# One level of Strassen's scheme for the last two token chunks of a fused attention and gated feed-forward kernel

## The chip, the cores and the metric

The kernel runs on one core of a Trainium2 chip. The metric is the device time of one execution in microseconds (us). Three timed runs of the kernel before took 415.01, 415.22 and 415.52 us; their median is 415.22 us. Engines are named as in the profile: PE (TensorE matmuls), PEld (its weight loads), DVE (VectorE), ACT (ScalarE), POOL (GpSimd), SP (SyncE, here a DMA queue).

## The reference, cut to what matters

```python
# q, k, v: (8 batches, 8 heads, 1152, 64) float32
q_pool = q.reshape(B, H, S // 2, 2, D).mean(axis=3)           # 576 queries per head
attn   = softmax(q_pool @ k.T / sqrt(D))
x      = (attn @ v).transpose(0, 2, 1, 3).reshape(B * S // 2, 512)   # 4608 tokens
# w1, w2: (512, 1024); w3: (1024, 1024); w_out: (1024, 512)
out    = ((x @ w1) * (x @ w2)) @ w3 @ w_out                     # float32, (4608, 512)
```

## The kernel before, in words

**Attention.** Heads are worked in 32 pairs. Scores (`scores`, L422 to L436) go to PSUM, ACT takes their exponential into a ring buffer in SBUF (L436), and `av_mm` (L449 to L464) multiplies the ring by `v`. DVE normalises (`av_norm`, L479 to L499). For later pairs a DMA transpose on the SP queue writes the result into `xT` (L473), the transposed attention output with 512 features on 4 x 128 partitions and tokens along the columns; the 64 tokens that are left of each batch are turned on PE and copied by DVE (L517).

**Feed-forward.** The product T = w3 @ w_out is formed early in the kernel (`t_groups`, L527; matmuls of 256 columns at L544) and is kept in fp16 as `T16`. Tokens are worked in 9 chunks of 512 (`moe_groups`, L582 to L639). For each of 8 feature tiles `ft`, `proj` (L563 to L567) makes 4 matmuls of 512 columns with `w1`, then 4 with `w2`. The first product is copied out of PSUM (`asb`: L593 on ACT once attention is over, L595 on DVE before that), and DVE multiplies the second one with it into `gT` in fp16 (L599). Then each of the 4 tiles of 128 tokens takes 8 matmuls of 512 columns against `T16` (L610), is scaled out of PSUM half by DVE (L616) and half by ACT (L617), and is stored. The last tile is cut into 384 and 128 columns (L623 to L634).

**Order.** A planner (`_Plan`, `_visits`) searches, before the program is emitted, in what order scores, AV units and feed-forward steps go on PE while attention runs. A chunk is put into the queue when its tokens exist (`release`, L754). The chunks are numbered from 0. Chunk 6 is worked beside the last attention units; chunks 7 and 8 come after all of them, in the stretch where attention is over (`tail`, L806 on).

**Queues.** POOL makes the casts and pair sums of the inputs (L343, L347, L349, L356) and issues the stores of chunks that are worked during attention; SP issues loads, the transposes of `xT`, and the stores of the tail; ACT issues the last two. Each engine takes its instructions in program order. PSUM has 8 banks of 512 fp32 columns: three tiles `psc` of two banks, one `mo`, and one `avb`.

**Checks.** The softmax sums are checked on DVE (L816 to L822), one small matmul adds the result up (L827), and a register is loaded from it (`values_load`, L833) ahead of a general path that isn't taken here.

Of the kernel before, what the change touches and what calls it, by code (L numbers as in the profile page):

```python
# [8 lines left out]
FP32 = mybir.dt.float32  # L9
FP16 = mybir.dt.float16  # L10
AF = mybir.ActivationFunctionType
ALU = mybir.AluOpType
# [109 lines left out]
class _Plan:  # L122
# [62 lines left out]
    def copy(self):  # L185
        p = _Plan.__new__(_Plan)
        p.__dict__.update(self.__dict__)
        return p
# [63 lines left out]
REACH = 1.5  # L252


@with_exitstack
def kernel(
    ctx: ExitStack,
# [10 lines left out]
    nc = tc.nc  # L268
# [14 lines left out]
    QM = 4  # L283
# [29 lines left out]
    wosb = msb.tile([128, NF, dm], FP16)  # L313
# [108 lines left out]
    def scores(s):  # L422
        psc = ps.tile([128, 2, 512], FP32, tag="psc", bufs=3, name="psc")
        f = s * G
        while f < s * G + G:
            p, r = f // FLAT, f % FLAT
            jt, i0 = r // Sq, r % Sq
            ln = min(Sq - i0, s * G + G - f)
            kT2, qpT = pairs[p][:2]
            for u in range(2):  # L430
                nc.tensor.matmul(psc[:, u, f - s * G:f - s * G + ln],  # L431
                                 kT2[u * 64:u * 64 + 64, jt, :], qpT[u * 64:u * 64 + 64, i0:i0 + ln],
                                 start=True, stop=True)
            f += ln
        r0 = (s * G) % RING
        nc.scalar.activation(out=ring[:, :, r0:r0 + G], in_=psc, func=AF.Exp, bias=0.0, scale=SCALE)  # L436
# [129 lines left out]
                nc.tensor.matmul(pw[:, d0:d0 + n], wt[:, mc, ft * 128:ft * 128 + 128], xT[:, mc, a:a + n],  # L566
                                 start=(mc == 0 and d0 == 0), stop=(mc == NC - 1), skip_group_check=True)  # L567

    def store(eng, pos, osb):
        b, r = pos // (2 * Sq) * 2, pos % (2 * Sq)  # L570
        if r == QM * 128:
            for u in range(2):
                r0 = (b + u) * Sq + QM * 128
                eng.dma_start(out=out[r0:r0 + QT, :], in_=osb[u * QT:u * QT + QT, :])
            return
        if r > QM * 128:
            b, r = b + 1, r - QM * 128 - 2 * QT
        eng.dma_start(out=out[b * Sq:b * Sq + QM * 128, :].rearrange("(p c) n -> p c n", c=QM)[:, r // 128, :], in_=osb)  # L578

    final, near = [], [False]  # L580

    def moe_groups(c):  # L582
        t = {}

        def first(pa, ft):
            if ft == 0:
                t["g"] = msb.tile([128, NF, CH], FP16, tag="g8", bufs=2, name="gT")
            proj(pa, w1sb, ft, c)

        def keep(pa):  # L590
            t["a"] = msb.tile([128, CH], FP32, tag="asb", bufs=2, name="asb")
            if tail[0]:
                nc.scalar.copy(out=t["a"], in_=pa)  # L593
            else:
                nc.vector.tensor_copy(out=t["a"], in_=pa)  # L595

        for ft in range(NF):
            def gate(pb, ft=ft):
                nc.vector.tensor_tensor(out=t["g"][:, ft, :], in0=pb, in1=t["a"], op=ALU.mult)  # L599
# [3 lines left out]
        tts = list(range(0, CH, 128))  # L603
        if c in final:
            tts.sort(key=lambda tt: (c * CH + tt) % (2 * Sq) != QM * 128)
        for n, tt in enumerate(tts):
            def go(po, tt=tt, n=n):
                near[0] = c in final and n >= len(tts) - 3
                for ft in range(NF):
                    nc.tensor.matmul(po, t["g"][:, ft, tt:tt + 128], T16[:, ft, :],  # L610
                                     start=(ft == 0), stop=(ft == NF - 1))

            def put(po, tt=tt):
                osb = msb.tile([128, dm], FP32, tag="osb", bufs=3)
                if tail[0]:
                    nc.vector.tensor_scalar_mul(out=osb[:, 0:256], in0=po[:, 0:256], scalar1=1.0 / (SCL * SCL))  # L616
                    nc.scalar.mul(out=osb[:, 256:512], in_=po[:, 256:512], mul=1.0 / (SCL * SCL))  # L617
                    store(nc.scalar if c in final and tt == tts[-2] else nc.sync, c * CH + tt, osb)
                else:
                    nc.vector.tensor_scalar_mul(out=osb, in0=po, scalar1=1.0 / (SCL * SCL))  # L620
                    store(nc.gpsimd, c * CH + tt, osb)

            def go_last(po, tt=tt):  # L623
                osb = msb.tile([128, dm], FP32, tag="osb", bufs=3)
                for hs in (slice(0, 384), slice(384, dm)):
                    ph = ps.tile([128, 2, 512], FP32, tag="psc", bufs=3, name="mol")[:, 0, 0:hs.stop - hs.start]
                    for ft in range(NF):
                        nc.tensor.matmul(ph, t["g"][:, ft, tt:tt + 128], T16[:, ft, hs],
                                         start=(ft == 0), stop=(ft == NF - 1))
                    if hs.start:  # L630
                        nc.scalar.mul(out=osb[:, hs], in_=ph, mul=1.0 / (SCL * SCL))
                    else:
                        nc.vector.tensor_scalar_mul(out=osb[:, hs], in0=ph, scalar1=1.0 / (SCL * SCL))
                store(nc.scalar, c * CH + tt, osb)  # L634

            if c in final and n == len(tts) - 1:
                yield 2, go_last, None, 0.0
            else:
                yield 2, go, put, 0.0  # L639

    queue, ahead = [], []

# [89 lines left out]
    final.extend(loose[max(loose)])  # L732
    units = []
    for i, (p, t) in enumerate(UNITS):
        old = p - 1 if t == QM else p
# [18 lines left out]
    def release():  # L754
        for c in loose.get(avn[0], []):
            queue.append(moe_groups(c))
# [70 lines left out]
    nc.tensor.matmul(avb[0:1, 0:1], okh, ones, start=True, stop=True)  # L827
# [3 lines left out]
    while not near[0]:  # L831
        fill()
    bad = nc.values_load(badi[0:1, 0:1], min_val=0, max_val=128 * NQ)  # L833
    while fill():
        pass
    fast.close()
    with tc.If(bad > 0):
        _general(tc, q, k, v, out, w1sb, w2sb, T16)
# [30 lines left out]
```

## Time and profile before

| what | value |
|---|---|
| median of the timed runs | 415.22 us (415.01 to 415.52) |
| span of the profiled execution, first to last instruction | 414.1 us |
| what lies around the span, median less span (the profiled execution has no other time on record) | 1.1 us |
| PE busy over the span | 399.9 us (97%) |
| ACT, DVE, POOL busy over the span | 78%, 50%, 40% |
| matmuls of chunks 7 and 8 in the chain that ended last | 367.68 to 409.36 us of the span |
| last instruction that the trace lists | a store issued at 409.69 us, 0.42 us long |

Read the page from its part 4, the chain that ended last: it names the engine on which time can be won or lost. Busy times of the other engines show what they could still take. A matmul's listed duration holds the time until its end is modelled, so neighbours overlap; the distance from one start to the next is what it costs PE. In the groups, "128x512 f16" after the names is the operand on each partition, and "128*128" marks the full array.

### The profile page before, as it was taken

What the parts mean: (1) busy time and instruction counts of PE and PEld (TensorE: products, weight loads), DVE (VectorE), ACT (ScalarE), POOL (GpSimd) and SP (SyncE); (2) the same over time, 40 slices, a digit from 0 to 9 for tenths busy, and PEclk for the clock granted to TensorE, in tenths of its full rate; (3) what the DMA queues carried; (4) which work ended last, traced back from release to release, by engine and by line L of the source; (5) the groups of instructions that cost most, each with busy time, mean ns of one, the idle gap of its engine ahead of it and who ended that gap; (6) DMA issues with size and microseconds to landing.
All of it is one profiled execution on the core that took longest, in us unless ns stands there. A gap on an engine that the chain in (4) does not pass through costs nothing.

```text
span 414.1 us, 12744 instructions
## 1 busy us (share of the span) xinstructions
PE 399.9 (97%) x5337; PEld 246.9 (60%) x5337; DVE 205.5 (50%) x573; ACT 323.4 (78%) x353; POOL 167.6 (40%) x212
## 2 busy tenths in 40 slices
PE   3899999999999999999999999999999999999995
PEld 1477787565556655566556556655777655644442
DVE  1256665665356535554455436553556346744241
ACT  4878979898989998899999999999899986022321
POOL 4979976470655316504535155505532210010000
PEclk9999999999999999999999999999999999999999
DMA  8999999999799898959999999998975440030302
GB/s 263 210 320 289 269 286 312 348 247 265 185 238 252 221 286 278 242 70 278 273 264 280 264 252 270 292 260 163 303 207 121 85 90 15 16 114 2 101 0 108
DMA packets 90832, 86.34 MB, mean 209 GB/s; under 512 B 59664, under 2 KB 64272, under 8 KB 90768
## 3 DMA queue, kind: packets, MB, share of 16 engines
q1 hardware_dynamic: 81312, 58.80, 59.1%
q0 software_dynamic: 8880, 25.63, 21.6%
q10 hardware_dynamic: 576, 1.05, 0.8%
q8 instruction: 42, 0.69, 0.7%
q14 instruction: 22, 0.18, 0.1%
HBM read 67.11 MB, written 9.44 MB: 185 GB/s over the span
## 4 chain that ended last, share of the span: by engine, by line
PE 93%; ACT 2%; DMA 2%; DVE 1%; issue 1%; SPq 0%; POOL 0%; ACTq 0%
PE psc L431 20%; PE avb L462 17%; PE mot L566 16%; PE mo L566 15%; PE mo L610 11%; PE mot L610 5%; PE mo L544 3%; PE avb L459 3%; ACT ring L436 2%; PE ptk L371 2%; DMA kst<-in_k_dram 2%; DVE kqT L373 1%; PE mot L544 1%; PE mo L535 1%; PE mot L535 1%
## 5 line engine op out<-in xcount | busy, mean ns | idle before, releaser
L436 ACT ACTIVATE ring<-psc 128x1024 f16<-128x1024 f32 x324 | 308.3, 1025 | 33.8 <-PE psc L431 32.0
L462 PEld LDWEIGHTS <-ring 128*128 128x128 f16 x2304 | 84.4, 98 | 26.3 <-issue 7.1
L431 PE MATMUL psc<-kqT 64*128 64x512 f16 (+7 forms) x1152 | 96.2, 291 | 3.4 <-ACT ring L436 0.9
L462 PE MATMUL avb<-vaug,ring 128*128 128x65 f16 x2304 | 91.4, 193 | 0.0
L343 POOL CAST kq<-kst 128x1152 f16<-128x1152 f32 x31 | 35.7, 1150 | 74.3 <-DMA kqT<-kq 52.3
L431 PEld LDWEIGHTS <-kqT 64*128 64x128 f16 x1152 | 46.0, 95 | 31.0 <-issue 8.4
L578 POOL DMA_DIRECT2D out_dram<-osb x23 | 12.7, 551 | 101.6 <-DVE rzall L483 99.9
L610 PE MATMUL mo<-T,gT 128*128 128x512 f16 x192 | 45.6, 380 | 0.0
L566 PEld LDWEIGHTS <-w2sb 128*128 128x128 f16 x320 | 28.2, 98 | 28.3 <-issue 4.2
L566 PEld LDWEIGHTS <-w1sb 128*128 128x128 f16 x320 | 28.2, 98 | 27.7 <-issue 3.9
L610 PEld LDWEIGHTS <-gT 128*128 128x128 f16 x280 | 25.3, 98 | 32.2 <-issue 5.2
L483 DVE RECIPROCAL rzall<-avb 128x2 f32<-128x2 f32 x144 | 23.8, 165 | 37.0 <-PE avb L462 20.2
L566 PE MATMUL mot<-xT,w1sb 128*128 128x512 f16 (+2 forms) x172 | 41.1, 364 | 0.1
L620 DVE TENSOR_SCALAR osb<-mo 128x512 f32<-128x512 f32 x24 | 16.6, 692 | 48.5 <-PE mo L610 48.5
L347 POOL TENSOR_TENSOR kq<-qst 128x512 f16<-128x512 f32 x31 | 39.4, 1272 | 1.2 <-DMA qst<-in_q_dram 1.2
L566 PE MATMUL mot<-xT,w2sb 128*128 128x512 f16 (+2 forms) x156 | 38.0, 368 | 0.0
L356 POOL CAST vaug<-vst 128x1152 f16<-128x1152 f32 x32 | 36.6, 1143 | 2.6 <-DMA vst<-in_v_dram 2.5
L599 DVE TENSOR_TENSOR gT<-mot,asb 128x512 f16<-128x512 f32 x37 | 25.6, 692 | 22.0 <-PE mot L566 20.8
L599 DVE TENSOR_TENSOR gT<-mo,asb 128x512 f16<-128x512 f32 x35 | 24.2, 692 | 24.6 <-PE mo L566 24.4
L566 PE MATMUL mo<-xT,w2sb 128*128 128x512 f16 (+2 forms) x164 | 36.2, 349 | 0.0
L595 DVE COPY asb<-mo 128x512 f32<-128x512 f32 x32 | 22.1, 691 | 24.0 <-PE mo L566 23.7
L566 PE MATMUL mo<-xT,w1sb 128*128 128x512 f16 (+2 forms) x148 | 33.1, 351 | 0.0
(76 smaller groups left out, 287.4 us busy)
## 6 DMA issues: line engine op xcount, KB each, us to landing
vst<-in_v_dram SPq DMA_DIRECT2D x25, 576.0 KB, 4.9
kst<-in_k_dram SPq DMA_DIRECT2D x23, 576.0 KB, 5.9
qst<-in_q_dram SPq DMA_DIRECT2D x23, 512.0 KB, 7.2
out_dram<-osb POOLq DMA_DIRECT2D x23, 256.0 KB, 5.2
kst<-in_k_dram POOLq DMA_DIRECT2D x8, 576.0 KB, 9.8
qst<-in_q_dram POOLq DMA_DIRECT2D x8, 512.0 KB, 10.4
vst<-in_v_dram POOLq DMA_DIRECT2D x7, 576.0 KB, 7.2
w3c<-in_moe_w_dram POOLq DMA_DIRECT2D x4, 512.0 KB, 8.1
```

Source lines behind the costliest of these rows:

```text
L343: nc.gpsimd.tensor_copy(out=kq16[:, 0:NJ].rearrange("p c u d -> p u c d"), in_=kst.rearrange("p u (c d) -> p u c d", d=D))
L347: eng.tensor_tensor(out=kq16[:, NJ:NJ + QM].rearrange("p c u d -> p u c d"), in0=qv[:, :, :, 0], in1=qv[:, :, :, 1], op=ALU.add)
L356: nc.gpsimd.tensor_copy(out=va[:, :, :, 0:D], in_=vs.pop(p).rearrange("p u (c d) -> p u c d", d=D))
L431: nc.tensor.matmul(psc[:, u, f - s * G:f - s * G + ln], kT2[u * 64:u * 64 + 64, jt, :], qpT[u * 64:u * 64 + 64, i0:i0 + ln], start=True, s ...
L436: nc.scalar.activation(out=ring[:, :, r0:r0 + G], in_=psc, func=AF.Exp, bias=0.0, scale=SCALE)
L462: nc.tensor.matmul(avb[:, o + u * E1:o + u * E1 + E1], ring[:, u, c0:c0 + 128], va[:, u, jt, :], start=(jt == 0 and u == 0), stop=(jt == N ...
L483: nc.vector.reciprocal(out=rzall[:, i, :], in_=av[:, :, D:E1].rearrange("p u o -> p (u o)"))
L566: nc.tensor.matmul(pw[:, d0:d0 + n], wt[:, mc, ft * 128:ft * 128 + 128], xT[:, mc, a:a + n], start=(mc == 0 and d0 == 0), stop=(mc == NC - ...
L595: nc.vector.tensor_copy(out=t["a"], in_=pa)
L599: nc.vector.tensor_tensor(out=t["g"][:, ft, :], in0=pb, in1=t["a"], op=ALU.mult)
L610: nc.tensor.matmul(po, t["g"][:, ft, tt:tt + 128], T16[:, ft, :], start=(ft == 0), stop=(ft == NF - 1))
L620: nc.vector.tensor_scalar_mul(out=osb, in0=po, scalar1=1.0 / (SCL * SCL))
```

## The change

For chunks 7 and 8 alone, each of the three products (x with w1, x with w2, the gated result with T) is cut into 2 x 2 blocks and formed from 7 block products instead of 8 (Winograd's form of Strassen's scheme). With A the stationary side and B the moving side:

- sums of blocks: S1 = A21 + A22, S2 = S1 - A11, S3 = A11 - A21, S4 = A12 - S2; T1 = B12 - B11, T2 = B22 - T1, T3 = B22 - B12, T4 = B21 - T2
- products: P1 = A11 B11, P2 = A12 B21, P3 = S4 B22, P4 = A22 T4, P5 = S1 T1, P6 = S2 T2, P7 = S3 T3
- results: C11 = P1 + P2; u2 = P1 + P6; u3 = u2 + P7; C21 = u3 + P4; C22 = u3 + P5; C12 = u2 + P5 + P3

The sums of products are held in PSUM as far as they go: bank x of a set collects P1, P6, P7, P4; bank y gets a copy of P1 made by ACT, to which P2 is added; bank z collects P5 and P3. ACT copies u2 and u3 out to SBUF on the way, and DVE adds them to z for C12 and C22.

A **unit** is one block product of a set: 4 matmuls of 256 columns. There are 8 sets for the projections ("g", two chunks x two groups j of feature tiles x two weights w) and 4 for the product with T ("o", two chunks x two groups u of tokens), of 7 units each: 84 units. Sets with w = 0 leave fp32 results in SBUF; sets with w = 1 multiply theirs into `gT`, and then form the four sums of `gT` that the product with T needs. These multiplications out of SBUF and sums go to POOL where j is even, to DVE where j is odd (`side`).

Sums of the weights and of T (12 instructions of 1024 fp16 elements a partition, `weight_sums`) go to POOL after its last cast; sums of x (8 of 512 elements, `x_sums`) go to POOL after the last attention unit. The stores of chunks 5 and 6 go from the POOL queue to SP. The last chunk's first 256 tokens are stored in two column halves, one of them on the ACT queue for one tile. A new search (`_Late.order`) gives the order of the 84 units on PE and their banks. The small matmul of the check comes ahead of the 84 units, and its register is loaded 6 units before their end. The old last-tile split is gone.

```diff
+class _Late:
+    UNIT = 0.436
+    SEEN = {"act": 0.2, "dve": 0.2, "pool": 0.25}
+    AFTER = {1: (), 5: (), 6: (1,), 2: (1,), 7: (6,), 4: (7,), 3: (7, 5)}
...
+    def order(sets, full, width=60, look=3):
...
+                    cost = n.pe - n.work + 0.1 * max(0, n.eng["dve"] - n.pe - 0.5) + 0.05 * max(0, n.eng["act"] - n.pe - 0.5)
...
+                store(nc.sync if c >= LATE - 2 else nc.gpsimd, c * CH + tt, osb)
...
+    def weight_sums():
+        for w, tag in ((w1sb, "kst"), (w2sb, "vst")):
...
+            nc.gpsimd.tensor_tensor(out=s1, in0=a21, in1=a22, op=ALU.add)
+            minus(s2, s1, a11)
+            minus(s3, a11, a21)
+            minus(s4, a12, s2)
...
+    def late_chunks(before_end):
...
+        sets = [("g", j, w) for j in range(4) for w in range(2)] + [("o", c, u) for c in range(2) for u in range(2)]
+        order, bank = _Late.order(sets, (0, 2, 4))
...
+            pt = banks[bank[k, {1: "x", 6: "x", 7: "x", 4: "x", 2: "y", 5: "z", 3: "z"}[p]]]
+            for f, l in enumerate(left):
+                for i in range(kc):
+                    nc.tensor.matmul(pt[:, n * f:n * f + n], l[:, i, :], b[:, i, :],
+                                     start=(p in (1, 5) and f == 0 and i == 0), stop=(i == kc - 1), skip_group_check=True)
...
+            def plus(c, pz, u):
...
+                nc.vector.tensor_tensor(out=slot((k, c)), in0=pz, in1=at[k, u], op=ALU.add)
+                if gated:
+                    side.tensor_tensor(out=part(k[1] // 2, last, i, n), in0=flat(at[k, c]), in1=flat(at[a, c]), op=ALU.mult)
...
+            if p == 1:
+                nc.scalar.copy(out=banks[bank[k, "y"]][:, 0:w], in_=pt[:, 0:w])
...
+                for o, x, y, op in ((s1, g12, g22, ALU.add), (s3, g11, g12, ALU.subtract),
+                                    (s2, s1, g11, ALU.subtract), (s4, g21, s2, ALU.subtract)):
+                    side.tensor_tensor(out=o, in0=x, in1=y, op=op)
...
-        loose.setdefault(min(n, NU + 1), []).append(c)
+        if c < LATE:
+            loose.setdefault(min(n, NU + 1), []).append(c)
...
+                    weight_sums()
...
+    x_sums()
...
-    for _ in range(12):
-        fill()
+    while fill():
+        pass
     nc.tensor.matmul(avb[0:1, 0:1], okh, ones, start=True, stop=True)
...
+    late_chunks(lambda: bads.append(nc.values_load(badi[0:1, 0:1], min_val=0, max_val=128 * NQ)))
```

More of the change, by code (lines that the diff above doesn't have):

```diff
@@ L252, with __init__, copy, op @@
 REACH = 1.5
+class _Late:
+    UNIT = 0.436
+    SEEN = {"act": 0.2, "dve": 0.2, "pool": 0.25}
+    AFTER = {1: (), 5: (), 6: (1,), 2: (1,), 7: (6,), 4: (7,), 3: (7, 5)}
+    def __init__(self, full):
+        self.pe = self.work = 0.0
+        self.eng = dict.fromkeys(self.SEEN, 0.0)
+        self.at, self.bank = {}, {}
+        self.free = [0.0] * 8
+        self.full = frozenset(full)
+        self.past, self.key = None, frozenset()
+    def copy(self):
+        n = _Late.__new__(_Late)
+        n.__dict__.update(self.__dict__)
+        n.eng, n.at, n.bank, n.free = dict(self.eng), dict(self.at), dict(self.bank), list(self.free)
+        return n
+    def op(self, eng, after, took, name):
+        x = max(self.eng[eng], max(after) + self.SEEN[eng]) + took
+        self.eng[eng] = x
+        self.at[name] = x + 0.07
+    def room(self, written):
+        return [i for i in range(8) if self.free[i] < 1e8 and (i in self.full or not written)]
+    def take(self, who, written=False):
+        i = min(self.room(written), key=lambda i: (self.free[i], i in self.full, i))
+        x, self.free[i] = self.free[i], 1e9
+        self.bank[who] = i
+        self.full = self.full | {i}
+        return x
+    def give(self, k, role, name):
+        self.free[self.bank[k, role]] = self.at[k, name]
+    def wants(self, k, p):
+        x = [(k, n) for n in {6: ["y"], 2: ["y"], 7: ["u2"], 4: ["u3"], 3: ["c22"]}.get(p, [])]
+        if k[0] == "o":
+            n = {1: "g11", 5: "s1", 6: "s2", 2: "g21", 7: "s3", 4: "g22", 3: "s4"}[p]
+            x += [(n, 2 * k[1]), (n, 2 * k[1] + 1)]
+        return x
+    def start(self, k, p):
+        x = max([self.pe] + [self.at[w] for w in self.wants(k, p)])
+        return max(x, min(self.free)) if p in (1, 5) else x
+    def can(self, k, p):
+        at = self.at
+        if any((k, q) not in at for q in self.AFTER[p]) or any(w not in at for w in self.wants(k, p)):
+            return False
+        if p == 1 and (len(self.room(False)) < 3 or not self.room(True)) or p == 5 and not self.room(False):
+            return False
+        if k[0] == "g" and k[2]:
+            a = ("g", k[1], 0)
+            n = {2: "c11", 4: "c21", 3: "c12"}.get(p)
+            if n and (a, n) not in at:
+                return False
+            if p in (7, 5) and ((k, 7) in at or (k, 5) in at) and (a, "c22") not in at:
+                return False
+        return True
+    def go(self, k, p):
+        e = self.start(k, p) + self.UNIT
+        at, j = self.at, k[1]
+        self.pe, self.work = e, self.work + self.UNIT
+        at[k, p] = e
+        self.past, self.key = (self.past, (k, p)), self.key | {(k, p)}
+        gated = k[0] == "g" and k[2] == 1
+        act, dve = (0.6, 0.7) if k[0] == "g" else (0.4, 0.45)
+        a = ("g", j, 0)
+        side, add = ("dve", 0.42) if j % 2 else ("pool", 1.07)
+        def whole(c):
+            if gated:
+                self.op("dve", [e, at[a, c]], dve, ("g" + c[1:], j))
+                at[k, c] = at["g" + c[1:], j]
+            else:
+                self.op("act", [e], act, (k, c))
+        def plus(c, after):
+            self.op("dve", after, dve, (k, c))
+            if gated:
+                self.op(side, [at[k, c], at[a, c]], 0.75 if j % 2 else 1.3, ("g" + c[1:], j))
+        if p == 1:
+            self.take((k, "x"))
+            x = self.take((k, "y"), True)
+            self.op("act", [e, x], act, (k, "y"))
+        elif p == 5:
+            self.take((k, "z"))
+        elif p == 6:
+            self.op("act", [e], act, (k, "u2"))
+        elif p == 2:
+            whole("c11")
+            self.give(k, "y", "c11")
+        elif p == 4:
+            whole("c21")
+            self.give(k, "x", "c21")
+        elif p == 3:
+            plus("c12", [e, at[k, "u2"]])
+            self.give(k, "z", "c12")
+        else:
+            self.op("act", [e], act, (k, "u3"))
+        if p in (7, 5) and (k, 7) in at and (k, 5) in at:
+            plus("c22", [at[k, "u3"], at[k, 5]])
+        if gated and all((k, q) in at for q in self.AFTER):
+            for o, x, y in (("s1", "g12", "g22"), ("s3", "g12", "g11"), ("s2", "s1", "s1"), ("s4", "s2", "g21")):
+                self.op(side, [at[x, j], at[y, j]], add, (o, j))
+    @staticmethod
+    def order(sets, full, width=60, look=3):
+        beam = [_Late(full)]
+        for _ in range(7 * len(sets)):
+            new = {}
+            for s in beam:
+                seen = [k for k in sets if any((k, p) not in s.at for p in s.AFTER)][:look]
+                for k, p in [(k, p) for k in seen for p in s.AFTER if (k, p) not in s.at and s.can(k, p)]:
+                    if s.start(k, p) > s.pe + 1.5:
+                        continue
+                    n = s.copy()
+                    n.go(k, p)
+                    cost = n.pe - n.work + 0.1 * max(0, n.eng["dve"] - n.pe - 0.5) + 0.05 * max(0, n.eng["act"] - n.pe - 0.5)
+                    v = new.setdefault(n.key, [])
+                    v.append((round(cost, 4), len(v), n))
+            beam = sorted(((c, i, n) for i, v in enumerate(new.values())
+                           for c, _, n in sorted(v, key=lambda x: x[:2])[:2]), key=lambda x: x[:2])[:width]
+            beam = [x[2] for x in beam]
+        s = min(beam, key=lambda s: max(s.pe, s.eng["dve"], s.eng["act"]))
+        out, past = [], s.past
+        while past:
+            past, x = past
+            out.append(x)
+        return out[::-1], s.bank
@@ L312 @@
     w3c = [msb.tile([128, 4, dff], FP16, tag="g8", bufs=2, name=f"w3c{i}") for i in range(2)]
-    wosb = msb.tile([128, NF, dm], FP16)
+    wosb = msb.tile([128, NF, dm], FP16, tag="wo", bufs=1, name="wosb")
     ring = att.tile([128, 2, RING], FP16, tag="ring", bufs=1)
@@ L567, in proj, with store @@
                                  start=(mc == 0 and d0 == 0), stop=(mc == NC - 1), skip_group_check=True)
-    def store(eng, pos, osb):
+    def store(eng, pos, osb, cols=slice(0, dm)):
         b, r = pos // (2 * Sq) * 2, pos % (2 * Sq)
@@ L573, in store @@
                 r0 = (b + u) * Sq + QM * 128
-                eng.dma_start(out=out[r0:r0 + QT, :], in_=osb[u * QT:u * QT + QT, :])
+                eng.dma_start(out=out[r0:r0 + QT, cols], in_=osb[u * QT:u * QT + QT, :])
             return
@@ L577, in store @@
             b, r = b + 1, r - QM * 128 - 2 * QT
-        eng.dma_start(out=out[b * Sq:b * Sq + QM * 128, :].rearrange("(p c) n -> p c n", c=QM)[:, r // 128, :], in_=osb)
-    final, near = [], [False]
+        eng.dma_start(out=out[b * Sq:b * Sq + QM * 128, :].rearrange("(p c) n -> p c n", c=QM)[:, r // 128, cols], in_=osb)
     def moe_groups(c):
@@ L602, in moe_groups, with go @@
             yield 1, lambda pb, ft=ft: proj(pb, w2sb, ft, c), gate, 0.0
[L603 to L608, printed above, removed]
+        for tt in range(0, CH, 128):
+            def go(po, tt=tt):
                 for ft in range(NF):
@@ L617, in put @@
                     nc.scalar.mul(out=osb[:, 256:512], in_=po[:, 256:512], mul=1.0 / (SCL * SCL))
-                    store(nc.scalar if c in final and tt == tts[-2] else nc.sync, c * CH + tt, osb)
                 else:
                     nc.vector.tensor_scalar_mul(out=osb, in0=po, scalar1=1.0 / (SCL * SCL))
[L621 to L634, printed above, removed]
@@ L636, in moe_groups, with minus @@
-            if c in final and n == len(tts) - 1:
-                yield 2, go_last, None, 0.0
-            else:
-                yield 2, go, put, 0.0
+                store(nc.sync if c >= LATE - 2 else nc.gpsimd, c * CH + tt, osb)
+            yield 2, go, put, 0.0
+    HF, HM, HC = NF // 2, dm // 2, CH // 2
+    LATE = B * Sq // CH - 2
+    IS = 1.0 / (SCL * SCL)
+    wS, tS, xS = [], {}, {}
+    def minus(out, x, y):
+        nc.gpsimd.tensor_tensor(out=out, in0=x, in1=y, op=ALU.subtract)
@@ new lines, in x_sums @@
+    def x_sums():
+        st = msb.tile([128, 2, 4, NC // 2, HC], FP16, tag="wo", bufs=1, name="xS")
+        for c in (0, 1):
+            (_, a, n), = runs(LATE + c)
+            b11, b12 = xT[:, 0:NC // 2, a:a + HC], xT[:, 0:NC // 2, a + HC:a + n]
+            b21, b22 = xT[:, NC // 2:NC, a:a + HC], xT[:, NC // 2:NC, a + HC:a + n]
+            x1, x2, x3, x4 = (st[:, c, i] for i in range(4))
+            minus(x1, b12, b11)
+            minus(x2, b22, x1)
+            minus(x3, b22, b12)
+            minus(x4, b21, x2)
+            xS[c] = {1: b11, 2: b21, 3: b22, 4: x4, 5: x1, 6: x2, 7: x3}
@@ L730 @@
                     n = max(n, i + 2, index[(p, QM - 1)] + 1 + HELD if p >= XD and t < QM else 0)
-        loose.setdefault(min(n, NU + 1), []).append(c)
-    final.extend(loose[max(loose)])
+        if c < LATE:
+            loose.setdefault(min(n, NU + 1), []).append(c)
     units = []
@@ L830 @@
                             op0=ALU.mult, op1=ALU.add)
[L831 to L835, printed above, removed]
+    bads = []
+    late_chunks(lambda: bads.append(nc.values_load(badi[0:1, 0:1], min_val=0, max_val=128 * NQ)))
+    bad, = bads
     fast.close()
```

111 lines of the change are left out of this document (added).

## The prediction

> **What bounds the kernel now.** I read the page from its part 4, the chain that ended last.
>
> ```profile
> span 414.1 us, 12744 instructions
> ...
> PE 399.9 (97%) x5337; PEld 246.9 (60%) x5337; DVE 205.5 (50%) x573; ACT 323.4 (78%) x353; POOL 167.6 (40%) x212
> ...
> PE 93%; ACT 2%; DMA 2%; DVE 1%; issue 1%; SPq 0%; POOL 0%; ACTq 0%
> ```
>
> PE carries 93% of the chain, so an edit that takes work off PE is worth its whole length, as long as nothing else becomes late. Then the same chain in order of time, for the stretch that the change touches:
>
> ```profile
> 362.50 5.18 PE mot L610 x24
> 367.68 8.63 PE mot L566 x40
> 376.31 0.10 PE avb L827
> 376.41 5.29 PE mot L566 x24
> 381.69 6.91 PE mot L610 x32
> 388.60 13.81 PE mot L566 x64
> 402.42 5.18 PE mot L610 x24
> 407.60 1.76 PE mol L628 x16
> 409.36 0.02 issue
> 409.38 0.28 ACT osb L631
> ```
>
> The second number is the length of a piece. The 24 matmuls at 362.50 are the end of chunk 6. Chunk 7 is 40 + 24 projections and 32 matmuls with T, chunk 8 is 64, 24 and 16. The pieces join without a gap: each matmul of 512 columns costs 13.81 / 64 = 0.216 us, and PE waits for nobody. Last, the table of stages, from 390 to 400 us:
>
> ```profile
> 390.00:400.00 10.00, 10.00 (x48) 4.54 (x47) 4.15 (x6) 3.15 (x7) 0.00 (x0) 1.00 0.11 26
> ```
>
> The columns after the length are PE, PEld, DVE, ACT and POOL busy, the granted clock and the DMA share. DVE is busy 42%, ACT 32%, POOL not at all: there is room beside PE, and the change fills it.
>
> **What PE saves.** Removed: 409.36 - 367.68 - 0.10 (the check's matmul, which stays) = 41.58 us. Added: 84 units of 4 matmuls with 256 columns. The formation of T early in the kernel has just such matmuls, each with a fresh 128x128 weight:
>
> ```profile
> L544 PE MATMUL mo<-wosb,w3T x104: 272/273/283, 23.9 to 66.2; 128*128 128x256 f16 x104
> ```
>
> The 273 ns hold the drain; in the chain 8 of them take 0.87 us when they follow other full-array work, so 0.435 us a unit and 84 x 0.435 = 36.54 us. The weight loads double per column but fit: 98 ns each beside a pitch of 109 ns. Saving on PE: **41.58 - 36.54 = 5.04 us**. It is the ceiling of the gain.
>
> **What is added beside PE.** Operations at the rows' durations; 512 fp32 columns out of PSUM:
>
> ```profile
> L599 DVE TENSOR_TENSOR gT<-mot,asb 128x512 f16<-128x512 f32 x16 | 11.1, 692 | 17.3 <-PE mot L566 16.3 <-PE avb L827 1.0
> L593 ACT COPY asb<-mot 128x512 f32<-128x512 f32 x16 | 9.4, 585 | 16.2 <-PE mot L566 16.2
> ```
>
> One chunk's projections are 4 sets (j even and odd, w = 0 and 1), 28 units, 12.18 us of PE.
>
> - ACT: 5 copies for each w = 0 set (P1 to bank y, u2, u3, C11, C21), 3 for each w = 1 set: 16 x 0.585 = 9.4 us. The copy into PSUM isn't in this trace; below it lies the 0.478 us of an ACT copy of 384 columns, above it the 1.025 us of the exponential of 1024. I take 0.585, the row of the same size; its four copies a chunk change little (from -0.4 to +1.8 us of ACT's 2.8 us of slack).
> - DVE: 2 additions for each w = 0 set, 4 operations for each w = 1 set, 12 in all, and for the odd j two multiplications and four fp16 additions of 512 elements with both inputs in SBUF. 18 x 0.692 = 12.5 us by durations; in the trace two such operations in a row start 0.61 us apart (348.75 and 349.36), so 18 x 0.61 = 11.0 us. The fp16 addition has no row at 512 elements: at most it is L599's 0.692, and from below L616's 0.425 for 256 elements, as if half of them were free. I take 0.61, L599 in a row, since a check operation of two SBUF inputs (L818, 288 elements, 459 ns) shows the same rate of one element a cycle.
> - POOL, for the even j: 6 operations of 512 elements at L347's 1.272 us, 7.6 us.
>
> In the Trainium skill, VectorE: DVE Perf Modes, the section on the perf-mode tier table gives two-input operations on 16-bit SBUF data twice the fp32 rate. By it the four additions would cost about 0.43 us each (an estimate from that page and L599), DVE would need about 10.2 us, and the clump below would shrink by about half. No run here shows it yet; my sum goes by L599's row.
>
> So DVE has 11.0 us of work in 12.18 us of PE time where it had 42%. It comes in clumps: beside the last set of an odd j runs a set of the next pair, and the two hold 12 DVE operations, 7.3 us at 0.61 or 8.3 us at 0.692, against 14 units, 6.1 us, of PE. The surplus of 1.2 to 2.2 us occurs twice, at the ends of the two odd j's. DVE takes its queue in order, so behind the side operations stand the additions that let P3 go (C22) and that free PSUM banks; PE waits for those. Two sets hold 6 of 8 banks, so PE can run ahead by little. Between nothing and 4.4 us is lost; I take **1.5 us**, somewhat above half of the lower surplus for each.
>
> The round trips themselves should hide. A set's longest chain is P1, copy by ACT, P6, u2 by ACT, P7, u3 by ACT, C22 on DVE, P3: four units (1.74 us), three ACT steps of 0.21 (from PE's last issue, 370.10, to ACT's start, 370.31) + 0.585 + some 0.07 us, 2.6 us, and one DVE step, 0.97 us: 5.3 us. Two sets in turn give 6.1 us of PE work. So an order that alternates two sets covers it, by 0.8 us; one set alone would not (3.05 us).
>
> **The start.** Chunk 6 frees its last bank at 368.56 (ACT, L617 at 368.18 + 0.38), its others by 367.33; four units can go at 367.68 into other banks, to 369.4, while ACT makes the first copy for bank y by 369.2. Nothing lost. The check's matmul is moved ahead of the units; its input is ready at 366.57 (L822). No cost.
>
> **Sums on POOL.** POOL casts its last `v` at 327.72 and then only stores. L347 and L349 (512 elements 1.272 us, 128 elements 0.450 us) give 2.14 ns an element, so 2.37 us for 1024 and 28.4 us for the 12 weight sums: 328.9 to 357.3 us. The sums of x for chunk 7 need DVE's copy of 357.77 + 0.28, and four of 1.27 us end at 363.1, 4.6 us before the first use. For chunk 8 they wait for the transpose issued at 363.1 and landing 2.4 us later, and end near 370; they are used from 367.68 + 12.18 = 379.9. Hidden twice over; at double price the weight sums would end at 386 and cost some 18 us, but POOL's binary operations show 1259 to 1288 ns over the whole run, beside a busy DVE. Stores of chunks 5 and 6 go past SP's transposes: one store issue of 0.36 to 0.42 us ahead of the transpose of 363.1, against 9 us of slack. No cost.
>
> **The end.** The last result goes through DVE (0.425 us, L616) where ACT took 0.278 us: +0.15 us. The two last sets can end unevenly by a link of the chain, 0 to 0.7 us. The register load now comes where ACT and DVE have short idle times; before, it lay beside idle stretches of 1.3 us, so it costs 0 to 1 us. The last store's landing, 2.0 to 2.7 us in the rows of stores, stays. I take **0.5 us**, of 0.15 to 1.85.
>
> **Sum**, against the profiled execution: -5.04 + 1.5 + 0.5 = -3.0 us, span 414.1 to 411.1. The median of the runs is 1.1 us above the span; so 415.2 - 3.0 = **412.2 us**. Bounds of the terms: 410.3 (0.15 us in all) to 416.4 us.
>
> **The rivals.**
>
> A. The forecast: PE's saving less stalls, 412.2 us; own range 410.3 to 414.3. Chance 0.58.
>
> D. All hidden: the search finds an order without a stall, and DVE is faster than its row: 415.2 - 4.7 = 410.5 us. For it: the loads on ACT (77%) and POOL. Against it: DVE at 90%. Chance 0.12.
>
> B. ACT's queue is late. Behind each other stand copies of two sets; if a copy on the chain waits for one other (0.585 us) once in each of the 8 projection sets, 4.7 us go, and 0.3 us of gain less 0.5 at the end leave 415.4 us, no change. For it: the cover is only 0.8 us a pair of sets. Against it: ACT is idle a quarter of the time. Chance 0.14.
>
> C. DVE and POOL get in each other's way. The trace of before has no DVE operation with two SBUF inputs beside a busy POOL (both of L399 and the one of L818 run while POOL makes none). The change has 12, and POOL is at work 2 x 7.6 of 24.4 us, 62%. If such an operation waits until POOL's ends, it waits 0.62 x 0.64 = 0.4 us on average, 4.7 us in all, on an engine that has no slack: 412.2 + 4.7 = 416.9 us, slower. It decides from 3.0 / 12 = 0.25 us a piece. For it: POOL's work of the even j reaches into DVE's of the odd j, 6 us later. Against it: about half of DVE's would fall past POOL's end. Chance 0.16.
>
> On C: the Trainium skill, SBUF — State Buffer, the section on who interferes with whom, says that VectorE's second SBUF port pair is GpSimd's too, locked for a whole instruction, and that VectorE with two SBUF inputs counts. It is a rule against this change; no run here shows it yet.
>
> That the change doesn't do what it says could only be if 256 columns cost more than half of 512; L544 speaks against that.
>
> **Numbers.** About 0.2%, 0.8 us, is what a measurement of this kernel can tell from none. Faster: A 0.58, D 0.12, B 0.02 = 0.72. Same: B 0.09. Slower: C 0.16, B 0.03 = 0.19. The range, 410.2 to 416.2, leaves out most of C, and holds the terms' bounds but for 0.2 us.
>
> **What would show it.** Right: units start 0.435 us apart for most of 36.5 us; gaps on PE, 2 us in all, sit behind DVE at the ends of odd j's; POOL's sums of x end by 371. C shows as DVE operations at L347-like lengths or idle time ahead of them that ends with POOL; B as PE waits for ACT spread over all sets; the start is wrong if the first unit begins after 368. The forecast fails if PE's gaps pass 4 us.

## The result and the profile after

The changed kernel takes 427.45 us (426.58 to 427.93), the kernel before 415.24 us beside it: a ratio of 1.0295, interval 1.028 to 1.0309. It is slower by about 12 us, where 3 us less were forecast. Its profiled execution took 427.57 us with a span of 425.8 us.

The page of the changed kernel: the span, the busy times, and the shares of the chain that ended last.

```profile
span 425.8 us, 13106 instructions
...
PE 398.8 (94%) x5473; PEld 260.2 (61%) x5473; DVE 217.0 (51%) x593; ACT 336.1 (79%) x381; POOL 212.2 (50%) x237
...
PE 88%; ACT 4%; DVE 3%; issue 1%; DMA 1%; ACTq 0%; DVEq 0%
```

PE lost 5% of the chain, and ACT and DVE took it over: PE now waits for them. The chain in order of time, the first part of the late units (start, length, what):

```profile
362.72 5.18 PE mot L744 x24
367.90 0.09 PE avb L1114
367.99 1.43 PE lt L840 x12
369.43 0.44 PE lo L840 x4
369.86 0.45 PE lt L840 x4
...
370.39 0.59 ACT room L894
...
371.03 0.61 PE lt L840 x4
...
371.66 0.59 ACT room L876
...
372.30 1.10 PE lt L840 x8
```

Chunk 6 ends at 367.90, 0.2 us later than before, so almost nothing was lost up to there. Four matmuls of 256 columns follow each other in 0.436 us, as forecast. But already the seventh unit waits until a copy by ACT (L894, u2) has ended, and the ninth for another (L876, C11). The table of stages, from 390 to 400 us (PE, PEld, DVE, ACT and POOL busy, granted clock, DMA share):

```profile
390.00:400.00 10.00, 7.53 (x64) 6.23 (x64) 6.29 (x12) 4.71 (x9) 1.27 (x1) 1.00 0.01 2
```

Nobody is full: PE 75%, DVE 63%, ACT 47%, at the full clock. That is a kernel that waits for round trips, not one with a new bound. The list of waits, for PE alone from 367.9 us on (who waited for whom, us in total, times, longest):

```profile
PE lt L840 <- ACT room L894: 3.4, 6, 0.8
PE lt L840 <- ACT lt L899: 1.9, 3, 0.7
PE lt L840 <- DVE room L888: 1.9, 3, 1.0
PE lt L840 <- ACT room L876: 1.7, 3, 0.8
PE lt L840 <- DVE room L884: 1.1, 2, 0.9
PE lt L840 <- ACT room L878: 0.5, 1, 0.5
```

Eighteen waits, and all of them by units that write a tile `lt`; none by a unit that writes `lo` or `avb`. The tiles `lt` hold two banks each, `lo` and `avb` one. The theory below came from this list. It adds up to 10.5 us, because it counts from the listed end of a matmul, which holds its drain; by the starts of its matmuls PE stands 14.1 us, in 21 gaps.

Where the 11.7 us of span went: from the first unit at 367.93 to PE's listed end at 418.88 there are 50.95 us, where chunks 7 and 8 took 41.6 before. Without waits, 84 units of 0.4366 and the drain of the last (0.17) are 36.8 us. So the products did save 4.8 us, 14.1 us of waits came, and the end grew by 2.2 us, from 4.76 (409.34 to 414.10) to 6.93 (418.88 to 425.80). With chunk 6's end, 0.2 - 4.8 + 14.1 + 2.2 = 11.7 us.

### The profile page after: what moved, and what is told of

The parts are those of the page before. It is cut to its first block, busy times and chain, and to the rows that moved or that the text cites. A ratio compares the mean times of both kernels' runs of the same rounds, so it can differ in the third digit from the quotient of the medians.

```text
span 425.8 us, 13106 instructions
## 1 busy us (share of the span) xinstructions
PE 398.8 (94%) x5473; PEld 260.2 (61%) x5473; DVE 217.0 (51%) x593; ACT 336.1 (79%) x381; POOL 212.2 (50%) x237
## 4 chain that ended last, share of the span: by engine, by line
PE 88%; ACT 4%; DVE 3%; issue 1%; DMA 1%; ACTq 0%; DVEq 0%
PE psc L571 20%; PE avb L602 17%; PE mo L706 14%; PE mo L744 10%; PE mot L706 9%; PE lt L840 6%; PE mo L684 3%; PE avb L599 2%; ACT ring L576 2%; PE mot L744 2%; PE ptk L511 2%; ACT room L894 1%; DMA qst<-in_q_dram 1%; ACT lt L899 1%; DVE gT L874 1%
## 5 line engine op out<-in xcount | busy, mean ns | idle before, releaser
L718 POOL DMA_DIRECT2D out_dram<-osb x18 | 9.9, 552 | 56.3 <-DVE rzall L623 56.3
L744 PEld LDWEIGHTS <-gT 128*128 128x128 f16 x224 | 19.8, 98 | 25.6 <-issue 5.2
L706 PEld LDWEIGHTS <-w2sb 128*128 128x128 f16 x256 | 21.9, 97 | 20.8 <-issue 4.2
L706 PEld LDWEIGHTS <-w1sb 128*128 128x128 f16 x256 | 22.0, 97 | 20.3 <-issue 4.1
L637 DVE TENSOR_TENSOR xb<-avb,rzall 128x128 f16<-128x128 f32 x96 | 28.0, 292 | 3.3
L706 PE MATMUL mot<-xT,w1sb 128*128 128x512 f16 (+1 forms) x108 | 24.7, 355 | 0.1
L706 PE MATMUL mot<-xT,w2sb 128*128 128x512 f16 (+1 forms) x92 | 21.6, 361 | 0.0
```

The source lines that it names most:

```text
L637: nc.vector.tensor_tensor(out=xbt, in0=av[:, :, 0:D], in1=rzall[:, i, :].unsqueeze(2).to_broadcast([128, 2, D]), op=ALU.mult)
```

## The experiments

**Theory 1, pairs.** A unit that writes one bank of a two-bank tile also waits until ACT or DVE has read the *other* bank of that tile. In the changed kernel's program, 33 of the 84 units carry a wait for a read that touches only the neighbouring bank. In the trace, 19 of PE's 21 gaps, 13.7 of the 14.1 us, stand before units of these 33; the other two are 0.2 us each. The order found by the search, and the forecast, treat eight banks as independent. **Theory 2** (rival B): the round trips themselves are too long, ACT's queue is late. **Theory 3** (rival C): DVE and POOL hold each other up.

All of them, with the kernel before on the same chip each time. "PE" is from the first unit to PE's listed end, "end" from there to the end of the span:

| run | median us | before | ratio (interval) | PE | end |
|---|---|---|---|---|---|
| the changed kernel | 427.45 | 415.24 | 1.0295 (1.028 to 1.0309) | 51.0 | 6.9 |
| own_bank_tiles | 415.40 | 415.78 | 0.9977 (0.994 to 1.0014) | 37.3 | 8.1 |
| pair_tiles_new_pool | 434.63 | 415.78 | 1.0456 (1.0417 to 1.0495) | 55.0 | 7.1 |
| one_psum_tile | 412.97 | 415.78 | 0.9929 (0.9902 to 0.9955) | 37.3 | 7.7 |
| order_knows_pairs | 418.87 | 415.78 | 1.0092 (1.0065 to 1.012) | 41.7 | 8.2 |
| before_one_psum_tile | 414.81 | 415.31 | 0.998 (0.9961 to 0.9998) | 41.7 | 5.5 |
| one_tile_stores_off_sp | 412.55 | 415.31 | 0.9936 (0.992 to 0.9953) | 37.3 | 7.2 |
| after_stores_off_sp | 427.32 | 415.31 | 1.0332 (1.0267 to 1.0396) | 51.0 | 7.3 |
| after_sides_on_dve | 429.04 | 415.31 | 1.0325 (1.0304 to 1.0346) | 53.9 | 8.1 |
| one_tile_stores_act | 411.50 | 415.43 | 0.9911 (0.9886 to 0.9935) | 37.3 | 6.4 |
| one_psum_tile_again | 412.69 | 415.43 | 0.9936 (0.9915 to 0.9958) | 37.3 | 7.9 |

**own_bank_tiles: the same order and instructions, each bank a tile of its own.**

```diff
-        banks = [x for _ in range(3) for t in [ps.tile([128, 2, 512], FP32, tag="psc", bufs=3, name="lt")]
-                 for x in (t[:, 0, :], t[:, 1, :])]
-        banks += [ps.tile([128, 512], FP32, tag="mo", bufs=1, name="lo"), avb]
+        psx.close()
+        ps2 = fast.enter_context(tc.tile_pool(name="ps2", bufs=1, space=bass.MemoryType.PSUM))
+        banks = [ps2.tile([128, 512], FP32, tag=f"b{i}", name=f"lb{i}") for i in range(8)]
+        banks = [banks[i] for i in (2, 3, 6, 7, 4, 5, 1, 0)]
```

> The changed kernel with one edit: the eight PSUM banks of the late units are eight tiles of one bank each (a new pool, opened when the old one is closed) in place of three tiles of two banks, one "mo" and avb; the banks are physically the same ones, and order, engines and sums are those of the change. Theory 1 (a wait that the program adds between the two banks of one tile: a unit into bank y waits until ACT or DVE has read bank x of the same tile, and the other way round, which costs most of PE's 14 us of gaps): 411.5 to 414.0 us, the units within 38 to 40 us, with 0.9 us lost at the start because the new pool waits for the old one's last reader. Theory 2 (rival B of the prediction: ACT's own round trips and queue are late): ACT has the same instructions, so 425 to 429 us. Theory 3 (rival C: DVE and POOL hold each other up): the same engines do the same work, so 425 to 429 us.

**pair_tiles_new_pool: the control.** The same new pool, but four tiles of two banks.

```diff
+        two = [ps2.tile([128, 2, 512], FP32, tag=f"b{i}", name=f"lb{i}") for i in range(4)]
+        banks = [t[:, i, :] for t in two for i in range(2)]
```

> The control for the kernel with eight tiles: the same new pool and the same late start, but four tiles of two banks each. Theory 1: the waits inside a tile are back, for one more pair (banks "mo" and avb too): 427 to 432 us. Theories 2 and 3: as the other one, within 1 us of it. If the pool itself were the cause, this kernel would be as fast as the one with eight tiles.

Measured: 415.40 and 434.63 us. The chain of own_bank_tiles:

```profile
368.09 31.18 PE lb L842 x284
...
399.34 0.37 ACT lb L901
...
399.75 3.65 PE lb L842 x32
...
403.44 1.49 PE lb L842 x12
```

The chain stays on PE for 71 units and then passes through a copy by ACT. By the starts of its matmuls, PE stands only twice, 0.2 us each, before the 73rd and the 81st unit. With one-bank tiles no unit's program wait is for another bank, and the time is level with the kernel before. With four pairs 42 units have such a wait, PE's waits are 13.2 us in the list, and the kernel is slower than the changed one, whose two single tiles are free of it. Theories 2 and 3 expected no such gain: ACT and DVE do the same work in both. The run missed theory 1's 411.5 to 414.0 us by 1.4 us. The first unit waits 0.8 us for chunk 6's last copy (`PE lb L842 <- ACT osb L752: 0.8, 1, 0.8`), which the expectation had counted with 0.9; but the end is 8.1 us long, 1.2 us more than in the changed kernel.

**one_psum_tile: all of PSUM as a single tile of eight banks, of which the old tiles are slices.**

```diff
-    avb = ps.tile([128, 512], FP32, tag="av", bufs=1)
+    eight = ps.tile([128, 8, 512], FP32, tag="all", bufs=1, name="eight")
+    avb = eight[:, 0, :]
...
-        psc = ps.tile([128, 2, 512], FP32, tag="psc", bufs=3, name="psc")
+        psc = psc_tile()
```

`psc_tile` hands out banks 2 and 3, 4 and 5, 6 and 7 of `eight` in turn; `mo` is bank 1.

> The changed kernel with all of PSUM as one tile of eight banks from the start of the program, of which scores, attention and late units take views; in this form the program has no wait between two different banks, and there is no change of pools. Theory 1: 0.5 to 1.2 us below the kernel with eight one-bank tiles, 410.8 to 413.2 us, the units starting at 367.9 us as in the changed kernel. Theories 2 and 3: 425 to 429 us.

Measured: 412.97 us, and in the second run 412.69 us. Its late units, start to the last (the columns as in the stage table above):

```profile
366.30:403.20 36.90, 36.81 (x336) 32.54 (x336) 25.48 (x45) 24.77 (x53) 16.30 (x14) 1.00 0.15 51
```

And of the changed kernel, for the same instructions:

```profile
368.00:418.90 50.90, 40.20 (x336) 32.40 (x336) 26.03 (x45) 25.29 (x53) 15.78 (x14) 1.00 0.13 44
```

The counts in brackets are equal: 336 matmuls, 45 DVE, 53 ACT and 14 POOL instructions, with DVE and ACT busy the same 25 to 26 us. Only the waits differ, 14 us of them. In the list of PE's waits of one_psum_tile there is no line of a late unit at all; by the starts PE stands twice, 0.2 us each, for ACT (L907 and L904). So a wait for the neighbour isn't a matter of a tile being larger than a bank: with eight banks in one tile, one unit has it, and PE doesn't stop there. Why the program gets it for tiles of two banks and not for one of eight, no run here tells.

> The changed kernel with all of PSUM as one tile, once more, beside the kernel before on the same chip: 412.5 to 413.5 us, 0.5 to 0.9% below the kernel before.

**order_knows_pairs: the pairs kept, but the search knows of them.**

```diff
+            i = self.bank[k, {6: "x", 7: "x", 4: "x", 2: "y", 3: "z"}[p]]
+        return max(x, self.busy[i ^ 1]) if i < 6 else x
```

> The changed kernel with its tiles as they are, but the search for the order takes into account that a unit waits for the readers of the other bank of its tile. Theory 1: the waits stay but fall beside other units where the search can arrange it; better than the changed kernel by 4 to 10 us, 417 to 424 us, and worse than with no such wait. Theory 2: the number of ACT's copies and their chain are the same, 425 to 429 us. Theory 3: 425 to 429 us.

Measured: 418.87 us (421.03 in the profiled execution, where chunk 6 ends at 369.4, 1.5 us later than in the changed kernel). The kept sums use 19 slots in turn, and in this order the slots of five values are written again before the values are read, or by the very instruction that reads them. So the output of this kernel is wrong, and its time only tells what the order does; instructions and sizes are the same. By the ratios (1.0295 to 1.0092) the planner's ignorance cost some 8.4 us, and with the waits known 0.9% of loss against before is left. A part of it is rival C, which shows itself here. Side sums on DVE, then on POOL (start, length):

```profile
394.49 2.07 DVE L936 TENSOR_TENSOR room<-gT 128x512 f16<-128x512 f16 x2
396.47 1.37 DVE L936 TENSOR_TENSOR room<-room,gT 128x512 f16<-128x512 f16 x1
397.88 1.26 DVE L936 TENSOR_TENSOR room<-gT,room 128x512 f16<-128x512 f16 x1
```

```profile
393.49 2.78 POOL L936 TENSOR_TENSOR room<-gT 128x512 f16<-128x512 f16 x2
396.23 1.33 POOL L936 TENSOR_TENSOR room<-room,gT 128x512 f16<-128x512 f16 x1
397.64 1.21 POOL L936 TENSOR_TENSOR room<-gT,room 128x512 f16<-128x512 f16 x1
```

The four DVE sums take 2.07 + 1.37 + 1.26 = 4.70 us; undisturbed ones take 0.42 each, 1.68. The last two end 0.28 and 0.29 us after the POOL sum beside them (397.84 after 397.56, 399.14 after 398.85): each lasted until POOL was done. The four together take 3.0 us too long, and the chain of this kernel runs through them.

**after_sides_on_dve: rival C taken away from the changed kernel.**

```diff
-            side = nc.vector if last else nc.gpsimd
+            side = nc.vector
```

> The changed kernel with all side sums and products of the late sets on DVE, none on POOL, so that DVE and POOL do not meet there. If DVE and POOL holding each other up is the main cause of the loss, most of it goes: 412 to 417 us. If the waits between the banks of a tile are, PE's gaps stay: 426 to 432 us, since only about 1.1 us of prolonged DVE work goes, and about 6 operations of 0.42 to 0.69 us for each even j come to DVE, which then has some 17 us for 24 us of units.

Measured: 429.04 us. All 8 multiplications of L890 now last 0.692 us, where in the changed kernel those on DVE went up to 1.37:

```profile
L890 DVE TENSOR_TENSOR gT<-room x8: 692/692/693, 375.3 to 410.4; 128x512 f16<-128x512 f32 x8
```

The prolonged operations are gone and the lost time isn't: PE's waits for ACT are the same 3.4, 1.9 and 1.7 us, and those for DVE's L888 grow from 1.9 to 3.1. Theory 3 falls as the cause.

**before_one_psum_tile: the control for the best layout.** The kernel before, with the edit of one_psum_tile.

> The kernel before, with all of PSUM held as one tile of eight banks and nothing else changed: a control for the gain of the changed kernel in one tile. If what that gained came only from the waits between the two banks of a tile in its late units (the theory of the pairs), the kernel before has nothing to gain from one tile: 415.0 to 416.0 us, and chunk 6 ends at 367.5 to 367.9 as before. If the one tile itself also takes waits out of the stages ahead, as chunk 6's end at 366.22 there instead of 367.68 suggests, this kernel ends 1 to 1.7 us earlier: 413.8 to 414.8 us.

Measured: 414.81 us, 0.2% less than before. Its chain from the end of chunk 6 on:

```profile
361.22 5.18 PE eight L618 x24
366.40 8.63 PE eight L574 x40
...
406.31 1.76 PE eight L636 x16
```

And one_psum_tile, the end of chunk 6 with the check's matmul in its chain, and the last two units in its timeline (listed to 403.51):

```profile
366.22 0.10 PE eight L1122
...
402.48 1.04 PE L848 MATMUL eight<-T,room 128*128 128x256 f16 x8
```

Chunk 6 ends at 366.40, 1.3 us earlier than before, as in one_psum_tile, and the end takes 0.7 us longer. So the one tile has a small gain of its own: 414.81 us lies at the upper edge of the 413.8 to 414.8 us expected for that, and the interval, 0.9961 to 0.9998, only just leaves out no gain at all. Where ahead of chunk 6 it comes from was not traced further. From chunk 6's end to PE's listed end, the check's matmul included, there are 41.67 us here (366.40 to 408.07) and 37.29 us in one_psum_tile (366.22 to 403.51): with free banks **the scheme saves 4.4 us on PE**, or 4.8 without its two stops of 0.2 us, against 5.04 forecast.

**The end: three runs.** In one_psum_tile 7.7 us lie between PE's listed end and the end of the span. Theory E: SP issues the last stores, and only then goes to its closing part. From the trace's records of SP, which the views above don't print (start, what):

```
kernel before          408.07 branch   410.59 first step after it   414.1 end   (last store issued 409.69, by ACT)
changed kernel         419.37 branch   422.39 first step after it   425.8 end   (last store issued 419.37, by ACT)
one_psum_tile          404.93 branch   407.69 first step after it   411.2 end   (last store issued 404.01, by ACT)
one_tile_stores_act    402.78 branch   405.79 first step after it   409.6 end   (last store issued 405.07, by ACT)
```

Behind SP's branch lie 2.5 to 3.0 us without an instruction, then 3.4 to 3.9 us of semaphore steps, one by one, some of which wait. In the kernel before, the gap is hidden beside the last stores. On this the Trainium skill, Runtime: NRT & Kernel Launch, the section on instruction fetch mechanics, says that a taken branch to a page that isn't loaded makes the engine fetch it by DMA first; a few packets of the instruction queues do move in that time in the trace, but whose they are it doesn't tell, and no run here takes the branch away.

```diff
-                store((nc.sync, nc.scalar)[k[2]] if n else nc.sync, pos, row[:, n * HM:n * HM + HM],
+                store(nc.scalar if n else nc.sync, pos, row[:, n * HM:n * HM + HM],
...
-                store(nc.sync, pos, row)
+                store(nc.gpsimd if k[1] == 1 else nc.sync, pos, row)
```

> The changed kernel in one PSUM tile, with the stores of the last chunk's rows for i = 1 issued by POOL and both second halves of C12's by ACT, so that SP's last issue comes earlier. The theory that the end grew because SP, which issues the last stores, only then goes through its closing branch (7.2 us from SP's last issue to the span's end, against 4.4 us from the last store to the end of the kernel before) expects 2 to 2.8 us less than the same kernel without this edit: 410.2 to 411.2 us. If the end grew because of the last link on ACT and DVE or the last store's landing, the edit changes nothing: 412.6 to 413.4 us.

> The changed kernel with that edit of the stores alone, its pairs of banks as they were. By the theory of the end: 424.6 to 425.6 us, 2 to 2.8 us less than the changed kernel, and the gaps on PE (about 14 us from chunk 6's end to the last unit) unchanged. By its rival: 427 to 428 us.

Measured: 412.55 and 427.32 us. Theory E's 2 to 2.8 us did not come; the medians are 0.4 us and 0.1 us lower, inside the spread of both, and the ratios to the kernel before on the same chip are no lower (0.9936 against 0.9929, 1.0332 against 1.0295). In the trace of one_tile_stores_off_sp SP did go on earlier (first step after the branch at 404.51 instead of 407.69), but then waited for the last store to land (407.39), and POOL's closing drain lasted to 409.60. POOL has such a drain behind its last instruction in every run, 5.0 to 5.6 us long where it issues no late store: in one_psum_tile it starts at 396.23 and is over long before the end. Here it starts behind POOL's stores, at 403.69, and lasts 5.9 us, 2.6 us past their landing (407.02). So the edit took one late end away and brought another.

```diff
-                store(nc.gpsimd if k[1] == 1 else nc.sync, pos, row)
+                store(nc.scalar if k[1] == 1 and k[2] == 1 else nc.sync, pos, row)
```

> The changed kernel in one PSUM tile; of the last chunk's stores, the second full row and both halves of the C12's are issued by ACT, POOL issues none, SP only the first full row and what comes before it. In the run with stores on POOL the end went from SP's walk after its last issue to the landing of the last store and to POOL's drain, 5.9 us long. If these three ends lie within 1 us of each other, as that trace shows, taking both SP's and POOL's away leaves the landing and is worth 0.7 to 1.3 us against one PSUM tile alone: 411.6 to 412.3 us. If the end grew for one reason, SP, alone, this gains the 2 to 2.8 us that were expected there: 410.2 to 411.0 us. If store issues by ACT are slow (1.1 to 1.7 us for the second of two in a row in the runs with two there), nothing is gained: 412.7 to 413.4 us.

Measured: 411.50 us, 1.2 us below one_psum_tile on the same chip (412.69), and the fastest kernel of the study (ratio 0.9911, interval 0.9886 to 0.9935, which just overlaps that of one_psum_tile there). The end is 6.4 us. The gain lies at the edge of what three ends within 1 us of each other give. What is left of the end is the stores:

```profile
402.39 0.34 SPq L726 DMA_DIRECT2D out_dram<-room  x1
402.83 2.81 ACTq L726 DMA_DIRECT2D out_dram<-room  x3
402.86 0.86 DVE L892 SCALAR_TENSOR_TENSOR room<-eight,room 128x256 f32<-128x256 f32 x2 [0.67 <-PE eight L848]
```

DVE is done at 403.72, but ACT's three issues end at 405.64: one of them took 1.66 us instead of 0.36. The end is still 0.9 us longer than that of before_one_psum_tile (5.5 us); how the rest divides between SP's closing part and the stores, no run shows.

## Why the prediction was wrong

- **The failed step** is "The round trips themselves should hide." It counted 5.3 us of round trip against 6.1 us of PE work of two sets, and "Two sets hold 6 of 8 banks, so PE can run ahead by little" took banks as independent. With one-bank tiles or one tile that is what happens: 37.3 us of PE and two stops of 0.2 us. In the changed kernel's two-bank tiles a set's x and y, or two sets, share a tile, and a unit waits for a read in the other bank: 13.7 of 14.1 us, where the forecast's own sign of failing was 4 us of gaps. A reader of the program could have seen it, since each unit's waits are fixed before it runs; the profile of before could not show it, as there no pair has its two banks filled and read apart.
- **PE's saving** was right: 5.04 forecast, 4.8 measured without the stops; a unit 0.4366 us against 0.435.
- **Stalls of 1.5 us at the ends of odd j's** were wrong in place and size. With free banks 0.4 us is lost in all, in two stops near the end that wait for ACT. The 0.61 was read from a multiplication followed by a copy (L599, then L595), not from two multiplications; two of those do start 0.61 apart in the changed kernel (L874 and L888, 401.29 and 401.90). The clumps of DVE work are smaller than thought, since the fp16 addition of 512 elements takes 0.418 to 0.425 us. So with free banks rival D's reason, a DVE faster than its row, is nearest to what the trace shows. The estimate of 0.43 us from the Trainium skill (VectorE: DVE Perf Modes, the perf-mode tier table) agrees with the trace.
- **Rival C** was a real mechanism with a small price here. The Trainium skill, SBUF — State Buffer, who interferes with whom, agrees with the trace: DVE's operations with two SBUF inputs end only after the POOL operation beside them, by 0.55 us in the changed kernel (387.85 after 387.30). There two of L890's four take 1.07 and 1.37 us, 1.1 us of DVE too much in all; in one_psum_tile it happens too, and no wait of PE in its list comes of it. It gave the right sign for a wrong reason.
- **Rival B**, ACT late, fell: with free banks the same 53 ACT instructions hold PE twice, 0.2 us each.
- **The start** was right: the first unit at 367.93, no wait before the seventh.
- **POOL's sums** were right to be hidden, at prices too high: 2.12 us for 1024 elements against 2.37, 1.15 for 512 against 1.27; the weight sums run from 320.5 to 345.8 us, the sums of x end at 369.3.
- **The end**, 0.5 us with at most 1.85, measured 2.2 us in the changed kernel and 2.2 us in one tile (7.7 against 5.5). The forecast priced the last step on DVE, an uneven end, the register load and the last store's landing, and not what each engine still does after its last instruction; 1.3 to 1.5 us went when the stores were moved to ACT.

With the pairs gone, the scheme is worth 0.4 to 0.5%, about 2 us, by the ratios (0.9929 and 0.9936 against 0.998 for the kernel before in one tile, each known to 0.2 or 0.3%), and with its stores moved 0.7%. The forecast of 3.0 us less comes near the last, in part by luck: it put 1.5 us on stalls, where 0.4 came with free banks, and 0.5 us on the end, where 2.2 came with the stores as they were. Only the saving on PE was sized right.

## What to carry to other kernels

Before you count on a buffer as free, read which waits the program really holds: a wait can be for a neighbour in the same tile, and then every cover that was worked out bank by bank is void. A planner must know the same granularity as the program, or the tiles must be cut as the planner thinks. And a list of waits in which one tile's name stands on every line and its neighbours' on none was worth more here than any sum of busy times.

## What the runs showed of the hardware

- Store issues on SP and ACT mostly take 0.33 to 0.6 us. Among the last stores, one that starts 0.1 to 0.3 us behind another on its queue took 1.10 to 2.07 us in eight of the ten runs with the 84 units. It isn't the nearness alone: earlier ones just as near took 0.38 to 0.73 us. What it is stays open.
- POOL's drain behind its last instruction lasted 5.0 to 5.6 us in the runs where POOL issues no late store, wherever it came, and 5.9 and 6.7 us where POOL had issued the last rows' stores.
- ACT copies 512 fp32 columns from PSUM to PSUM in 0.57 to 0.59 us, the same as from PSUM to SBUF (0.585).
- Where DVE's operation with two SBUF inputs meets a sum on POOL, POOL is slowed as well: 1.48 us instead of 1.15 (L919), and 1.33 (L936).
